# Token tiles 2 and 3 by one transposing load instead of TensorE turns, at the start of a gated mixing kernel

## The chip, the cores and the metric

The kernel runs on one core of a Trainium2 chip. The metric is the device time of one execution in microseconds (us), the median of several runs. Beside it there is one profiled execution of the kernel before, with its own time; every duration below comes from that one.

## The reference: what is computed

For 2048 tokens `x` of width 512 (32 heads of 16) two branches are computed and mixed with a gate per token. All inputs are bf16; the entries are small random numbers.

```python
g = sigmoid((x * gate_w).sum(-1, keepdims=True))
# branch A: linear attention with a learned feature map, wqkv = [wq | wk | wv]
q, k, v = split(x @ wqkv)                       # 32 heads of 16
pq, pk = q @ w_phi[h], k @ w_phi[h]             # per head, 16x16
phi = concat(softmax(p), softmax(-p))           # 32 features per head
kv, z = sum_s phi_k * v, sum_s phi_k            # over all 2048 tokens
a = ((phi_q @ kv) / (phi_q . z + 1e-6)) @ wo
# branch B: a dense layer with relu
b = relu(x @ w1) @ w2                           # 512 -> 1376 -> 512
return g * a + (1 - g) * b
```

## The kernel before

**A list of tasks with a fixed order.** Every piece of work is a named task (`add`, line 93) on one engine: SP, POOL, ACT, DVE or PE. The order of the tasks on each engine is written out by hand in `ORDER` (lines 17 to 62); `emit` (line 133) walks through an engine's string, waits for the tasks that the next one depends on, and issues it. An engine never overtakes: whatever stands behind a waiting task waits too. The `dur`, `lat` and `boost` numbers at the tasks are a planner's costs and priorities; they take no part when the kernel runs, since the order is given. `g.follow` only asserts an order.

**Layout.** `XT` holds x transposed: 128 partitions, 4 row steps (of the 512 input columns), 2048 tokens. It is filled in four chunks of 512 tokens. Chunks 1 to 3 come by transposing loads (`load_t`, line 276: `x1`, `x2`, `x3`, lines 308 to 311), which read token rows from memory and write them turned. Chunk 0, four tiles of 128 tokens, comes otherwise: `load_x` (line 287) fetches the rows of tile m plainly into `XN` (a piece of the later buffer `FT`), TensorE turns each 128x128 block by a matmul against the identity (`pe_xt`, line 348, tasks `xt{m}{n}`, two blocks each), and ACT (n = 0) and DVE (n = 1) copy the result from PSUM to `XT` (tasks `xe{m}{n}`, lines 361 to 366; 128x256 elements each).

**The start.** The first tasks of the SP queue are the loads `x00 w1a0 w1a2 x02 x03 w1b wphi wkT w1c wv x1 x2 wqT x3`; those of ACT's queue are `x01 w1a1 w1a3`. `w1a0` to `w1a3` are the four row steps of the first 512 columns of W1 (128 KB each), `w1b` the next 512 columns, `wphi` the 16x16 maps, `wkT` the key weights by a transposing load. `x1` waits until `w1c` has landed.

PE starts with `warm0` (line 257), six matmuls of 512 columns on constants whose result nobody reads. Then come `xt00 xt01 xt10 xt11`, the turns of tiles 0 and 1, and the W1 products of these two tiles: `hh00` (row step 0, tile 0), `hh01` (row step 0, tile 1), `hh1`, `hh2`, `hh3` (row steps 1 to 3, both tiles at once). Each is `pe_h_first` (line 401): four matmuls, one for each of the first four groups of 128 hidden columns, into four PSUM banks. Between `hh2` and `hh3` stand the turns of tiles 2 and 3, `xt20` to `xt31`. After `hh3` come `h0_0` to `h0_3` (`pe_h_rest`, line 407: the same four groups for tiles 2 and 3, four matmuls of 256 columns each), `h0_4`, `h0_5` (512 columns, these need `w1b`), and then `f1_0` to `f1_3` (`pe_fold`, line 372, L374): w_phi folded into the key weights, 16 matmuls, which need `wkT`.

**The rest.** From there on PE goes in its order through the W1 products `h{c}_{k}` (L397), values `v{m}` (L476), projections `pr_k`, `pr_q` (L496), sums over tokens `kv{m}` (L557), then per tile of 128 tokens the second dense layer `b{m}` (L622), the attention product `nd{m}` (L600) and the output product `a{m}` (L628). Between them POOL subtracts and multiplies for the softmaxes (L536, L550, L573; `t1`, `t2`, `nm` tasks), ACT exponentiates and empties PSUM, DVE reduces. Around the late PE tasks stand two small SP transposes per tile: `tq{m}` (L576) turns the query features from `FT` to `PHQ`, which `nd{m}` reads, and `to{m}` (L614) turns the attention result from `OTM` to `OT`, which `a{m}` reads. SP issues `tq0 tq1`, a gate store `g1_3`, then `to0 tq2`.

Of the kernel before, what the change touches and what calls it, by code (L numbers as in the profile page):

```python
# [18 lines left out]
        "x00 w1a0 w1a2 x02 x03 w1b wphi wkT w1c wv x1 x2 wqT x3 gw g1_1 g2_1 w2a g1_0 g1_2 w2b wo g2_0 tq0 tq1 "  # L19
        "g1_3 to0 tq2 tq3 to1 tq4 tq5 to2 to3 tq6 to4 tq7 g2_3 to5 g2_2 tq8 to6 tq9 to7 tq10 tq11 to8 to9 tq12 "  # L20
        "to10 tq13 tq14 to11 tq15 to12 to13 to14 to15 st15_1 "
    ),
    "pool": (
        "iota_r iota_i iota_c ones t1_k0 t2_k0 t1_k1 t2_k1 t2_k2 t1_k2 t1_k3 t2_k3 nm_k0 nm_k1 t1_k5 t1_k4 t2_k4 "
        "nm_k2 nm_k3 t1_k6 t1_k7 t2_k7 t2_k5 nm_k4 t1_k8 t2_k6 t2_k8 nm_k5 t2_q0 t1_q0 nm_k6 t2_q1 t1_q1 nm_k7 "
        "ra_q0 nm_q0 nm_k8 t2_q2 t1_q2 ra_q1 nm_q1 t1_q3 t2_q3 ra_q2 nm_q2 t1_q4 t2_q4 ra_q3 nm_q3 t1_q5 t2_q5 "
        "ra_q4 nm_q4 t2_q6 t1_q6 ra_q5 nm_q5 t2_q7 t1_q7 t2_q8 t1_q8 ra_q6 nm_q6 ra_q7 nm_q7 ra_q8 nm_q8 "
    ),
    "act": (
        "x01 w1a1 w1a3 xe00 xe10 xe20 xe30 rl0_0 rl0_1 rl0_3 rl0_2 fe1_1 fe1_3 rl0_5 rl0_4 ev_k0 rl0_8 rl0_6 "  # L30
        "rl0_7 ev_k1 rl1_0 rl0_9 ev_k2 rl1_1 ex_k0 ev_k3 rl1_3 rl1_2 ve0 rl1_5 ex_k1 rl1_4 ve1 ev_k4 rl1_6 rl1_7 "
        "ex_k3 rl1_8 ev_k5 ex_k2 ve2 rl0_10 rl1_9 ev_k6 rl1_10 ve3 rl2_0 rl2_1 ve4 ex_k4 rl2_2 ev_k7 rl2_3 rl2_4 "
        "ve5 rl2_6 rl2_5 rl2_7 ve6 rl2_8 rl2_9 rl2_10 ve7 ex_k5 ev_k8 ge1 ve8 ge0 ex_k7 rl3_0 rl3_1 ve9 ev_q0 "
        "ex_k6 ve10 gp0 ev_q1 rl3_3 ex_k8 gp1 rl3_2 rl3_4 ve11 ev_q2 ex_q0 rl3_5 ve12 ev_q3 ve13 rl3_6 ve14 ev_q4 "
        "rl3_7 ex_q1 rl3_8 ve15 rl3_9 rl3_10 ex_q2 ev_q5 ex_q3 ev_q6 oe0 ev_q7 ex_q4 oe1 st1 oe2 st0 oe3 ex_q5 "
        "ge3 ev_q8 oe4 st3 oe5 ge2 st2 ex_q6 gp2 oe6 ex_q7 st5 st4 ex_q8 st6 oe7 oe8 gp3 oe9 st7 oe10 st9 st10 "
        "oe11 st8 st11 oe12 oe14 st12 oe13 st14 st13 oe15_0 st15_0 "
    ),
    "dve": (
        "ident shift xe01 xe11 xe21 xe31 blk row4 wbd1 wbd3 mk wbd2 wbd0 fe1_0 fe1_2 mx_k0 mn_k0 mx_k1 mn_k1 "  # L40
        "mn_k2 mx_k2 mx_k3 mn_k3 sm_k0 rc_k0 sm_k1 rc_k1 mn_k4 mx_k4 mx_k5 sm_k2 gr0 rc_k2 gr1 mx_k6 sm_k3 rc_k3 "
        "mn_k7 sm_k4 mx_k7 rc_k4 mn_k5 gr2 fe0_0 fe0_1 fe0_2 fe0_3 mn_k6 mx_k8 mn_k8 sm_k5 rc_k5 mn_q0 mx_q0 "
        "sm_k6 rc_k6 sm_k8 go1 go0 sm_k7 mn_q1 mx_q1 rc_k7 sm_q0 mx_q2 rc_q0 rc_k8 mx_q3 mn_q3 mn_q2 mx_q4 sm_q1 "
        "kn1 kn0 kz0 kz1 rc_q1 mn_q4 gr3 rd0_1 rd0_0 o0_0 o0_1 sm_q2 rd1_0 rd1_1 rc_q2 mx_q5 o1_1 o1_0 mn_q5 "
        "rd2_0 rd2_1 o2_0 o2_1 sm_q3 rd3_1 rd3_0 rc_q3 o3_1 o3_0 mn_q6 rd4_1 o4_1 rd4_0 o4_0 sm_q4 rd5_0 rd5_1 "
        "rc_q4 o5_0 o5_1 mx_q6 rd6_1 rd6_0 o6_1 o6_0 sm_q5 rd7_1 rc_q5 o7_1 rd7_0 mx_q7 o7_0 mx_q8 mn_q8 mn_q7 "
        "rd8_0 rd8_1 o8_0 o8_1 sm_q6 rd9_1 rd9_0 rc_q6 o9_0 o9_1 rd10_1 rd10_0 o10_0 sm_q7 go2 o10_1 sm_q8 rd11_1 "
        "rd11_0 o11_0 rc_q8 o11_1 rc_q7 rd12_0 rd12_1 o12_1 o12_0 rd13_0 go3 rd13_1 o13_1 o13_0 rd14_0 rd14_1 "
        "o14_0 o14_1 rd15_0 rd15_1 o15_0 o15_1 oe15_1 "
    ),  # L50
    "pe": (
        "warm0 xt00 xt01 xt10 xt11 hh00 hh01 hh1 hh2 xt20 xt21 xt30 xt31 hh3 h0_0 h0_1 h0_2 h0_3 h0_4 h0_5 f1_0 "
        "f1_1 f1_2 f1_3 h0_6 pr_k0 h0_7 h0_8 pr_k1 h0_9 h1_0 pr_k2 h1_1 h1_2 pr_k3 h1_3 v0 h1_4 h1_5 v1 h1_6 "
        "pr_k4 h1_7 h1_8 v2 pr_k5 h1_9 kv0 h0_10 kv1 pr_k6 h1_10 v3 kv2 h2_0 h2_1 kv3 v4 pr_k7 h2_2 v5 h2_3 h2_4 "
        "h2_5 h2_6 h2_7 v6 h2_8 h2_9 h2_10 kv4 kv5 f0_0 kv6 f0_1 v7 f0_2 pr_k8 f0_3 h3_0 kv7 h3_1 v8 pr_q0 v9 "
        "h3_2 h3_3 v10 kv8 pr_q1 kv9 h3_4 v11 kv10 pr_q2 h3_5 kv11 v12 pr_q3 h3_6 v13 kv12 h3_7 v14 kv13 pr_q4 "
        "h3_8 h3_9 v15 kv14 h3_10 pr_q5 kv15 b0 nd0_0 nd0_1 b3 nd1_0 nd1_1 b2 pr_q6 a0 nd2_0 nd2_1 b1 nd3_1 pr_q7 "
        "nd3_0 b4 nd4_1 nd4_0 a1 pr_q8 nd5_1 a2 nd5_0 a3 b5 nd6_0 nd6_1 b7 nd7_0 nd7_1 a4 a5 b6 nd8_1 nd8_0 a6 b9 "
        "nd9_0 nd9_1 b8 nd10_0 nd10_1 a7 b10 nd11_1 a8 nd11_0 a9 b11 a10 nd12_0 nd12_1 b13 nd13_1 nd13_0 b12 "
        "nd14_0 nd14_1 b14 nd15_0 nd15_1 a11 a12 a13 a14 b15 a15_0 a15_1 "  # L60
# [88 lines left out]
def bass_gated_mix__linear_kernel_hedgehog__dense_activation_relu__prompt_kernel(  # L149
# [11 lines left out]
    x2 = A_x.rearrange("b s d -> (b s) d")  # L161
# [4 lines left out]
    P = 128  # L166
# [17 lines left out]
    WARM = (6 * (512,),)  # L184
# [3 lines left out]
    with ExitStack() as es:  # L188
# [98 lines left out]
        def load_x(m, eng, lat):  # L287
            load(f"x0{m}", eng, XN[:, m, :], x0r[:, m, :], dur=0.45, lat=lat)

        def load_w(j, eng, lat):  # L290
            load(f"w1a{j}", eng, W1[:, j, 0:512], w1r[:, j, 0:512], dur=0.45, lat=lat)

        load_x(0, "sp", 2.95)
        load_x(1, "act", 3.1)
        load_w(0, "sp", 3.2)
        load_w(1, "act", 3.4)
        load_w(2, "sp", 3.8)
        load_w(3, "act", 3.95)
        load_x(2, "sp", 4.0)
        load_x(3, "sp", 3.9)  # L300
        load("w1b", "sp", W1[:, :, 512:1024], w1r[:, :, 512:1024], dur=0.5, lat=5.0)
        load("wphi", "sp", WPS[:, :, :], A_w_phi.rearrange("(g hl) r c -> (hl r) g c", g=ND), dur=0.5, lat=4.9)
        load_t("wkT", WT[:, ND:2 * ND, :], A_wqkv[:, D:2 * D], (), 4.1, 2.7)
        load("w1c", "sp", W1[:, :, 1024:DFF], w1r[:, :, 1024:DFF], dur=0.5, lat=4.0)
        load("wv", "sp", WV[:, :, :], wvr, dur=0.5, lat=4.9)
# [40 lines left out]
        XB, FB = ((0, 1), (6, 7), (0, 1), (6, 7)), (0, 1, 6, 7)  # L346
# [7 lines left out]
        for m in range(4):  # L354
            for n in range(2):
                add(f"xt{m}{n}", "pe", lambda q, m=m, n=n: pe_xt(q, m, n),
                    (f"x0{m}", "ident", f"xe{m - 2}{n}" if m > 1 else None), dur=0.2, boost=9000.0 - 10 * m)
            for n, eng in enumerate(("act", "dve")):
                xo = XT[:, 2 * n:2 * n + 2, m * P:(m + 1) * P]
                xi = PS[:, XB[m][n], 0:2 * P].rearrange("p (j t) -> p j t", j=2)  # L360
                if eng == "act":
                    add(f"xe{m}{n}", eng, lambda q, o=xo, i=xi: q.activation(o, i, ACT.Copy), (f"xt{m}{n}",), dur=0.35,
                        boost=9000.0 - 10 * m)
                else:
                    add(f"xe{m}{n}", eng, lambda q, o=xo, i=xi: q.tensor_copy(o, i), (f"xt{m}{n}",), dur=0.37,  # L365
                        boost=9000.0 - 10 * m)
        x0 = [f"xe{m}{n}" for m in range(4) for n in range(2)]
# [10 lines left out]
        for j in range(ND):  # L378
            b = FB[j]
            war = [f"xe{2 + j // 2}{j % 2}"]  # L380
            add(f"f1_{j}", "pe", lambda q, j=j, b=b: pe_fold(q, 1, j, b), ("wkT", *wbd, *war), dur=0.24,
                boost=1800.0)
            evict(f"fe1_{j}", ("dve", "act")[j % 2], WP[:, 1, j, :], b, (f"f1_{j}",), boost=1800.0)
# [23 lines left out]
        def pe_h_rest(q, k):  # L407
            for j in range(ND):
                last = q.matmul(PS[:, GB4[k], 256:512], W1[:, j, k * P:(k + 1) * P], XT[:, j, 256:512],  # L409
                                start=(j == 0), stop=(j == ND - 1))  # L410
            return last
# [3 lines left out]
        add("hh00", "pe", lambda q: pe_h_first(q, 0, 0, P), ("xe00", "w1a0"), dur=0.22, boost=8500.0)  # L415
        add("hh01", "pe", lambda q: pe_h_first(q, 0, P, 2 * P), ("xe10", "hh00"), dur=0.22, boost=8500.0)
        prev = "hh01"
        for j in range(1, ND):
            add(f"hh{j}", "pe", lambda q, j=j: pe_h_first(q, j, 0, 2 * P), (f"xe0{j // 2}", f"xe1{j // 2}", f"w1a{j}", prev), dur=0.44,
                boost=8500.0)  # L420
            prev = f"hh{j}"
        for line in (("warm0", "xt00", "xt01", "xt10", "xt11", "hh00", "hh01", "hh1", "hh2", "xt20", "xt21", "xt30", "xt31",
                      "hh3"), ("xe00", "xe10", "xe20", "xe30"),
                     ("ident", "shift", "xe01", "xe11", "xe21", "xe31", "blk", "row4", "mk")):
            for a, b in zip(line, line[1:]):
                g.follow(a, b)
# [15 lines left out]
        for n, (kind, a, k) in enumerate(units):  # L442
            b = GB4[n] if n < 4 else HB[(n - 4) % len(HB)]
            if kind == "h":
# [5 lines left out]
                add(f"h{a}_{k}", "pe", lambda q, a=a, k=k, b=b, h=halved: pe_h_rest(q, k) if h else pe_h(q, a, k, b),  # L450
# [50 lines left out]
        for jn, (kind, tiles) in enumerate(jobs):  # L501
# [37 lines left out]
            if jn == NF - 2:  # L539
                war += [f"xt{m}{n}" for m in range(4) for n in range(2)]  # L540
# [200 lines left out]
```

## Time and profile before

| | us |
|---|---|
| median of 3 runs | 152.26 (151.87 to 152.49) |
| the profiled execution | 151.63 |
| its span, first to last instruction | 150.1 |
| PE busy | 145.3 (97%) |
| POOL, DVE, ACT busy | 109.4, 113.3, 92.2 |
| first turn on PE, `xt00` | starts at 3.57 |
| first product of tiles 2 and 3, `h0_0` | starts at 7.31 |

Times inside a profile count from the first instruction. 1.5 us of the profiled execution lie outside the span (151.63 less 150.1). In the timeline, a row gives start, duration, engine, line, operation, output<-input, shape and how many instructions of a kind were merged; in brackets stands the engine's idle time before the row and what ended it. "SPq" and "ACTq" rows are DMA issues: their duration is that of the issuing, not of the transfer. "PEld" is the loading of weights into TensorE, which runs beside its matmuls. A few matmul records are missing, which looks like a short idle stretch on PE that nothing ended.

### The profile page before, as it was taken

The page shows a single profiled execution, that of the slowest core. Times are in us where ns is not written, and L with a number is a line of the kernel's source. Part 1 is how long each engine was busy: PE and PEld are TensorE (multiplying, and loading weights), DVE is VectorE, ACT ScalarE, POOL GpSimd, SP SyncE. Part 2 cuts the span into 40 slices and gives each one's busy share as a digit, 9 for nine tenths or more (in the row PEclk, how much of TensorE's full clock was granted, in tenths as well). Part 3 has the DMA queues.
Part 4 walks back from the last instruction along what each step waited for, and adds up shares of the span by engine and source line. Part 5 has one row for each costly group of instructions (what it writes and reads, how often), then busy time and mean ns, then how long its engine had stood idle before and what let it go on. Part 6 is the DMA issues. An engine that isn't in the chain of part 4 may idle for free.

```text
span 150.1 us, 2498 instructions
## 1 busy us (share of the span) xinstructions
PE 145.3 (97%) x936; PEld 74.3 (49%) x953; DVE 113.3 (76%) x168; ACT 92.2 (61%) x127; POOL 109.4 (73%) x71
## 2 busy tenths in 40 slices
PE   7999999999999999999999999999999999999992
PEld 2774444445554465445444545455444454454461
DVE  2423666999899949969999999999999969436301
ACT  3356769799969766599983937446564551310151
POOL 3000499999999999999999999998999791330000
PEclk9999999999999999999999999999999999999999
DMA  4999991000005603400000230975659884766251
GB/s 144 302 261 239 163 231 23 0 0 0 7 1 112 238 0 54 120 0 0 4 0 0 60 82 15 116 159 135 174 106 155 195 213 105 146 171 144 65 163 52
DMA packets 46307, 15.59 MB, mean 104 GB/s; under 512 B 39796, under 2 KB 46292, under 8 KB 46296
## 3 DMA queue, kind: packets, MB, share of 16 engines
q1 hardware_dynamic: 43560, 12.99, 42.1%
q10 hardware_dynamic: 2736, 2.45, 5.0%
q8 instruction: 7, 0.11, 0.3%
q14 instruction: 4, 0.03, 0.1%
HBM read 4.42 MB, written 2.11 MB: 43 GB/s over the span
## 4 chain that ended last, share of the span: by engine, by line
PE 94%; DMA 2%; issue 1%; DVE 1%
PE PS L622 24%; PE PS L397 23%; PE PS L496 18%; PE PS L476 9%; PE PS L628 9%; PE PS L557 3%; PE PS L600 3%; DMA FT<-in_A_x_dram 2%; PE PS L643 2%; PE PS L409 1%; PE PS L374 1%; PE PS L403 1%; PE PS L350 1%; PE PS L654 1%; DVE XT L365 1%
## 5 line engine op out<-in xcount | busy, mean ns | idle before, releaser
L536 POOL TENSOR_TENSOR TS<-PB,MX 128x1024 bf16<-128x1024 bf16 (+1 forms) x18 | 30.8, 1719 | 14.9 <-DVE MX L527 14.9
L397 PE MATMUL PS<-XT,W 128*128 128x512 bf16 (+1 forms) x156 | 38.3, 379 | 0.2
L622 PE MATMUL PS<-W,HT 128*128 128x512 bf16 (+1 forms) x160 | 37.5, 379 | 0.3
L543 DVE TENSOR_REDUCE ZB<-FT 128x128 f32<-128x2048 bf16 (+1 forms) x18 | 36.5, 2030 | 0.7 <-ACT FT L541 0.6
L541 ACT ACTIVATE FT<-TS 128x2048 bf16<-128x2048 bf16 (+1 forms) x18 | 30.9, 1718 | 7.7 <-POOL TS L536 7.5
L536 POOL TENSOR_TENSOR TS<-MN,PB 128x1024 bf16<-128x1024 bf16 (+1 forms) x18 | 30.9, 1723 | 0.8 <-DVE MN L529 0.8
L496 PE MATMUL PS<-WP,XT 128*128 128x512 bf16 x124 | 30.0, 379 | 0.2
L550 POOL TENSOR_TENSOR FT<-FT,SC 128x2048 bf16<-128x2048 bf16 (+1 forms) x9 | 29.5, 3286 | 0.0
L454 ACT ACTIVATE HT<-PS 128x512 bf16<-128x512 f32 (+1 forms) x44 | 24.7, 597 | 6.1 <-PE PS L397 4.9
L622 PEld LDWEIGHTS PS<-W,HT 128*128 128x128 bf16 (+1 forms) x165 | 15.5, 98 | 17.1
L527 DVE TENSOR_REDUCE MX<-PB 128x64 bf16<-128x1024 bf16 (+1 forms) x18 | 19.5, 1084 | 5.8 <-ACT PB L523 5.7
L397 PEld LDWEIGHTS PS<-XT,W 128*128 128x128 bf16 (+1 forms) x160 | 15.6, 101 | 16.5
L673 ACT ACTIVATE OSB<-PS,OMG 128x512 bf16<-128x512 f32 x15 | 10.2, 686 | 22.1 <-PE PS L628 22.1
L529 DVE TENSOR_REDUCE MN<-PB 128x64 bf16<-128x1024 bf16 (+1 forms) x18 | 19.3, 1083 | 2.6 <-ACT PB L523 2.6
L523 ACT ACTIVATE PB<-PS 128x1024 bf16<-128x1024 f32 (+1 forms) x18 | 16.7, 926 | 6.4 <-PE PS L496 3.4
L496 PEld LDWEIGHTS PS<-WP,XT 128*128 128x128 bf16 x128 | 12.1, 98 | 13.9 <-DVE WP L344 0.4
L573 POOL TENSOR_TENSOR FT<-FT,SR 128x1024 bf16<-128x1024 bf16 (+1 forms) x9 | 15.6, 1735 | 0.7
L476 PE MATMUL PS<-WV,XT 128*128 128x512 bf16 x62 | 16.0, 379 | 0.1
L628 PE MATMUL PS<-WO,OT 128*128 128x512 bf16 x58 | 14.2, 378 | 0.1
L609 DVE SCALAR_TENSOR_TENSOR OTM<-PS,EG,RD 128x256 bf16<-128x256 f32 x32 | 13.8, 462 | 0.2
L607 DVE RECIPROCAL RD<-PS 128x16 f32<-128x16 f32 x32 | 6.5, 234 | 9.0 <-PE PS L600 8.8
L485 ACT ACTIVATE VS<-PS 128x512 bf16<-128x512 f32 x16 | 9.6, 602 | 4.8 <-PE PS L476 4.7
(50 smaller groups left out, 97.5 us busy)
## 6 DMA issues: line engine op xcount, KB each, us to landing
out_dram<-OSB ACTq DMA_DIRECT2D x15, 128.0 KB, 2.2
W<-in_B_w_dram SPq DMA_DIRECT2D x1, 1280.0 KB, 6.9
W<-in_B_w_dram SPq DMA_DIRECT2D x1, 512.0 KB, 4.6
WV<-in_A_wqkv_dram SPq DMA_DIRECT2D x1, 512.0 KB, 4.6
WO<-in_A_wo_dram SPq DMA_DIRECT2D x1, 512.0 KB, 5.1
FT<-in_A_x_dram SPq DMA_DIRECT2D x3, 128.0 KB, 3.2
W<-in_B_w_dram SPq DMA_DIRECT2D x1, 352.0 KB, 3.8
W<-in_B_w_dram ACTq DMA_DIRECT2D x2, 128.0 KB, 3.3
```

Of the source, the lines that this page charges most:

```text
L397: last = q.matmul(PS[0:m, b, :], W1[:, j, k * P:k * P + m], XT[:, j, chunk(c)], start=(j == 0), stop=(j == ND - 1))
L454: add(f"rl{a}_{k}", "act", lambda q, a=a, k=k, b=b, rows=rows: q.activation(HT[0:rows, k, chunk(a)], PS[0:rows, b, :], ACT.Relu), (prev,), ...
L476: last = q.matmul(PS[:, 2, :], XT[:, j, m * P:(m + 1) * P], WV[:, j, :], start=(j == 0), stop=(j == ND - 1))
L496: last = q.matmul(PS[:, n, :], XT[:, j, m * P:(m + 1) * P], WP[:, s, j, :], start=(j == 0), stop=(j == ND - 1))
L527: add(f"mx_{J}", "dve", lambda q, sl=sl, w=w, i=pbg: q.tensor_reduce(MX[:, sl, 0:w * H], i, AX.X, ALU.max), (f"ev_{J}", old("t1")), dur=0. ...
L529: add(f"mn_{J}", "dve", lambda q, sl=sl, w=w, i=pbg: q.tensor_reduce(MN[:, sl, 0:w * H], i, AX.X, ALU.min), (f"ev_{J}", old("t2")), dur=0. ...
L536: add(f"{tn}_{J}", "pool", lambda q, o3=o3, a3=a3, b3=b3: q.tensor_tensor(o3, a3, b3, ALU.subtract), (f"{'mx' if sg == 0 else 'mn'}_{J}", ...
L541: add(f"ex_{J}", "act", lambda q, fs=fs, ts=ts, w=w: q.activation(FT[:, fs, 0:w * F], TS[:, ts, 0:w * F], ACT.Exp), (f"t1_{J}", f"t2_{J}", ...
L543: add(f"sm_{J}", "dve", lambda q, fs=fs, sl=sl, w=w: q.tensor_reduce(ZB[:, sl, 0:2 * w * H], FT[:, fs, 0:w * F].rearrange("p (g d) -> p g ...
L550: add(f"nm_{J}", "pool", lambda q, f3=f3, sl=sl, w=w: q.tensor_tensor(f3, f3, SC[:, sl, 0:2 * w * H].unsqueeze(2).to_broadcast([P, 2 * w * ...
L622: last = q.matmul(PS[:, ab, :], HT[0:r, k, m * P:(m + 1) * P], W2[0:r, k, :], start=(k == 0), stop=False)
L628: last = q.matmul(PS[:, ab, :], OT[:, m % NOT, t, :], WO[:, t, :], start=False, stop=(t == ND - 1))
```

## The change

- The loads and turns of tiles 2 and 3 go: `x02`, `x03`, `xt20` to `xt31`, `xe20` to `xe31`. In their place there is one transposing load, `x023`, from 256 token rows straight into `XT`, in SP's queue behind `w1a2`.
- Tile 0's load `x00` becomes two loads of 64 rows each, `x00a` first in SP's queue and `x00b` first in ACT's, so that ACT issues four loads before anything else.
- The products of tiles 0 and 1 are split by tile for row step 1 as well: `hh10`, `hh11` in place of `hh1`. `hh01` stands behind the turns of tile 1 and behind `hh10`.
- The matmuls on constants are five of 512 columns and one of 256 ahead of the turns of tile 0 (`warm0`), and one of 256 columns between these turns and `hh00` (`warm1`).
- All five strings of `ORDER` are rewritten. Beside the names that go and come, tasks change places among their neighbours along the whole kernel: `h0_7` now stands ahead of `pr_k0`, `v0` ahead of `h1_0`, `kv14` and `h3_10` directly ahead of `kv15`. The order `b0, nd0, b3, nd1, b2, pr_q6, a0, nd2` on PE is as before; on SP the gate store `g1_3` moves from ahead of `to0 tq2` to behind them.
- The planner's numbers at the loads change with it; they have no part in the run.

```diff
     "sp": (
-        "x00 w1a0 w1a2 x02 x03 w1b wphi wkT w1c wv x1 x2 wqT x3 gw g1_1 g2_1 w2a g1_0 g1_2 w2b wo g2_0 tq0 tq1 "
-        "g1_3 to0 tq2 tq3 to1 ...
+        "x00a w1a0 w1a2 x023 w1b wphi wkT w1c wv x1 x2 wqT x3 gw g1_1 g1_0 g2_0 w2a w2b wo g2_1 tq0 tq1 to0 tq2 "
+        "g1_3 tq3 to1 ...
     "act": (
-        "x01 w1a1 w1a3 xe00 xe10 xe20 xe30 rl0_0 rl0_1 rl0_3 rl0_2 fe1_1 ...
+        "x00b x01 w1a1 w1a3 xe00 xe10 rl0_0 rl0_1 rl0_2 rl0_3 rl0_4 fe1_1 ...
     "pe": (
-        "warm0 xt00 xt01 xt10 xt11 hh00 hh01 hh1 hh2 xt20 xt21 xt30 xt31 hh3 h0_0 h0_1 h0_2 h0_3 h0_4 h0_5 f1_0 "
-        "f1_1 f1_2 f1_3 h0_6 pr_k0 h0_7 h0_8 pr_k1 h0_9 h1_0 pr_k2 ...
+        "warm0 xt00 xt01 warm1 hh00 xt10 xt11 hh10 hh01 hh11 hh2 hh3 h0_0 h0_1 h0_2 h0_3 h0_4 h0_5 f1_1 f1_2 f1_3 "
+        "f1_0 h0_6 h0_7 pr_k0 h0_8 h0_9 pr_k1 v0 h1_0 pr_k2 ...
-    WARM = (6 * (512,),)
+    WARM = (5 * (512,) + (256,), (256,))
-        load_x(0, "sp", 2.95)
-        load_x(1, "act", 3.1)
...
-        load_x(2, "sp", 4.0)
-        load_x(3, "sp", 3.9)
+        for n, eng in enumerate(("sp", "act")):
+            rows = slice(n * 64, n * 64 + 64)
+            load(f"x00{'ab'[n]}", eng, XN[rows, 0, :], x0r[rows, 0, :], dur=0.45, lat=1.95)
+        load_x(1, "act", 2.85)
...
+        load_t("x023", XT[:, :, 2 * P:4 * P], x2[2 * P:4 * P, :], (), 1.2, 3.0)
-        for m in range(4):
+        for m in range(2):
             for n in range(2):
                 add(f"xt{m}{n}", "pe", lambda q, m=m, n=n: pe_xt(q, m, n),
-                    (f"x0{m}", "ident", f"xe{m - 2}{n}" if m > 1 else None), dur=0.2, boost=9000.0 - 10 * m)
+                    (*(("x00a", "x00b") if m == 0 else (f"x0{m}",)), "ident"), dur=0.2, boost=9000.0 - 10 * m)
-        x0 = [f"xe{m}{n}" for m in range(4) for n in range(2)]
+        x0 = [*(f"xe{m}{n}" for m in range(2) for n in range(2)), "x023"]
-        add("hh00", "pe", lambda q: pe_h_first(q, 0, 0, P), ("xe00", "w1a0"), dur=0.22, boost=8500.0)
-        add("hh01", "pe", lambda q: pe_h_first(q, 0, P, 2 * P), ("xe10", "hh00"), dur=0.22, boost=8500.0)
-        prev = "hh01"
-        for j in range(1, ND):
+        for j in range(2):
+            for m in range(2):
+                add(f"hh{j}{m}", "pe", lambda q, j=j, m=m: pe_h_first(q, j, m * P, (m + 1) * P),
+                    (f"xe{m}0", f"w1a{j}", "hh00" if j + m else None, "hh01" if j + m == 2 else None,
+                     "hh10" if j + m == 2 else None), dur=0.22, boost=8500.0)
+        prev = "hh11"
+        for j in range(2, ND):
```

## The prediction

> **What bounds it now.** The page's busy shares come first: PE is busy for 97% of the span, and the chain that ended last is PE for 94%. The next question is whether PE ever waits, so the waits view comes next, for PE and for its weight loads (engine, line, waited for: total us, times, longest).
>
> ```profile
> PE PS L258 <- PEq L726: 0.8, 1, 0.8
> PE PS L409 <- DVE XT L365: 0.2, 1, 0.2
> ```
> ```profile
> PEld PS L350 <- DMA FT<-in_A_x_dram: 1.0, 1, 1.0
> PEld PS L409 <- ACT XT L362: 0.4, 1, 0.4
> PEld PS L496 <- DVE WP L344: 0.4, 1, 0.4
> PEld PS L600 <- DMA PHQ<-FT: 0.2, 1, 0.2
> ```
>
> Every wait of PE itself lies in the first 7.31 us; from `h0_0` (L409) to its end PE works without a stall. The other short gaps are missing records (L496: 124 matmuls, 128 weight loads). So the time is the moment at which `h0_0` starts, plus a fixed stretch of PE work, plus any new stall. The change can win only before `h0_0`, and the reordering behind it can only lose. The chain of waits up to there:
>
> ```profile
> 0.74 2.78 DMA FT<-in_A_x_dram
> 3.52 0.05 issue
> 3.57 0.97 PE PS L350 x8
> 4.53 0.30 PE PS L403 x4
> 4.83 0.03 issue
> 4.86 1.27 PE PS L403 x12
> 6.13 0.24 PE PS L350 x4
> 6.37 0.02 issue
> 6.40 0.78 DVE XT L365 x2
> 7.18 0.14 issue
> 7.31 1.91 PE PS L409 x16
> ```
>
> A load, turns, products, turns again, and at 6.37 the copies of tiles 2 and 3: their own load landed at 6.26 (issued at 2.63, 3.63 under way), just ahead of the last turns. The queues beside it:
>
> ```profile
> 2.15 0.91 SPq L272 DMA_DIRECT2D FT<-in_A_x_dram  x2
> 3.10 0.43 SPq L272 DMA_DIRECT2D W<-in_B_w_dram  x1
> 3.58 0.51 SPq L272 DMA_DIRECT2D WPS<-in_A_w_phi_dram  x1
> 4.13 3.54 SPq L277 DMA_TRANSPOSE WT<-in_A_wqkv_dram  x1
> ```
> ```profile
> 1.17 0.97 ACTq L272 DMA_DIRECT2D W<-in_B_w_dram  x2
> 2.17 1.28 ACT L362 ACT_TABLE_LOAD   x1 [2.17 <-issue]
> 4.00 0.81 ACT L362 ACTIVATE XT<-PS 128x256 bf16<-128x256 f32 x2 [0.55 <-PE PS L350]
> ```
>
> To be seen here: ACT loads its table only after its last DMA issue.
>
> **The start, step by step.** *Half loads.* The full tile took 2.78 us on SP and 2.98 (tile 1) on ACT. The windows view gives 349 GB/s for 3.57 to 4.39, so 64 KB less per queue, with two queues sharing, is 128 KB/349 = 0.37 us sooner: 3.15 to 3.3. The constants end at about 0.77 + 5 x 0.43 + 0.21 = 3.1. So `xt00` starts near 3.3, not 3.57.
>
> *ACT.* But ACT now issues four loads, so its table load starts 0.43 later, at 2.60, and ends at 3.88. `xe00` starts at 3.90 instead of 4.00, takes 0.38, and `hh00` starts 0.06 behind it: 4.34 instead of 4.44. The table load thus eats most of what the half loads bring. `w1a0` landed at 4.11 and has less ahead of it now.
>
> A rule speaks against the halves: the Trainium skill, "DMA: Bandwidth & Descriptors", section "Rules for kernel authors", says two transfers to disjoint partition halves aren't worth it, since they share the same engines. By that rule `xt00` stays at 3.57 and the gain below shrinks by the 0.10 of `hh00`; no run here shows it yet.
>
> *PE from `hh00` on.* Full-clock spacings: 0.056 to 0.06 us for 128 columns, 0.109 for 256. `hh00` takes 0.24 (0.05 more if its first matmuls still run at half speed): 4.63. `xt10`, `xt11`: 4 x 0.056, to 4.85. Tile 1 has landed (issued 0.43 later than before's 0.74, so 3.72 + 0.4 = 4.1). `hh10` runs to 5.08; `w1a1`, third on ACT's queue instead of second, lands 64 KB x 2 later, 4.31 + 0.37 = 4.68, in time. `hh01` needs `xe10`: first turn 4.63, copy 0.31 behind it (as 5.97 to 6.28 before), 0.38 long, 0.06 to the matmul: 5.38. Then `hh01` and `hh11` at 0.23 each, 5.84, and `hh2`, `hh3` at 0.435 each: 6.71. `w1a3` lands at 5.18 + 0.37 = 5.55, in time. So PE is ready for `h0_0` at 6.71 instead of 7.31: **0.60 us**. Gone are eight turns (0.45) and the wait for their copies (0.17 at PE); left is 0.3 of waiting for `xe10`.
>
> **The transposing load.** No row shows 256 token rows. Bounds: `x3` (512 KB, otherwise free queue) landed 4.45 after issue; half the bytes at the 278 GB/s of the window 13.60 to 14.80 (`x1`) is 0.94 less: 3.51, so 2.15 + 3.51 = 5.66. From above: `x2` took 5.91, so 8.06; `wkT` behind two loads took 5.62, so 7.77. I take the nearest row, the plain loads it replaces: same bytes, same place in the queue, landed at 6.26, plus 0.94 - 0.75 (256 KB at 349) = 0.19: 6.45. That leaves 0.26 before 6.71.
>
> *Behind it on SP* stand `w1b`, `wphi`, `wkT`. Its issue is half of `x1`'s 1.79, 0.9 us, what the two plain issues took together (0.91); at half of `wkT`'s 3.54 it is 0.9 longer. `w1b` landed at 7.70 and is needed at 6.71 + 1.75 = 8.46. `wkT` landed at 9.75; at the same rates it moves to 9.94, and `f1` wants it at 8.46 + 8 x 0.216 = 10.19. Slack 0.25; a late issue of 0.9 would make a stall of at most 0.65. `x1` landed at 17.13 and `h1_0` wants it near 18.7 as before, since `v0` now stands ahead of it.
>
> **The late part.** PE 0.60 earlier eats into slack everywhere. POOL begins its softmaxes after `pr_k0`, which has one unit more ahead of it (0.86) and so ends 0.26 later; POOL then works without a gap up to `nm_q1`, 92.21 + 0.26 = 92.47. The thinnest place is tile 2 (issues on SP, weight loads on PE):
>
> ```profile
> 92.37 1.20 SPq L614 DMA_TRANSPOSE OT<-OTM  x1
> 93.61 3.61 SPq L576 DMA_TRANSPOSE PHQ<-FT  x2
> ```
> ```profile
> 96.85 0.69 PEld L628 LDWEIGHTS PS<-WO,OT 128*128 128x128 bf16 x4 [0.17 <-issue]
> 97.77 0.40 PEld L600 LDWEIGHTS PS<-KVN,PHQ 128*128 128x128 bf16 x8 [0.22 <-DMA PHQ<-FT]
> ```
>
> `to0` (issued 92.37, 4.38 to landing) and `tq2` (93.61, 4.11) landed at 96.75 and 97.72, each just as PE asked. Others take 2.4 and 2.8: a 16 KB fetch of instructions at 94.38 lies in between. `tq2` was issued right behind `to0`, and `to0` hangs on `nd0` of PE, so both issues move forward with PE (91.77 and 93.0, past `nm_q1`): `nd2` wants data at 97.17, they land at 97.1 if 4.11 holds. I cost this at nothing; if the fetch holds the landing at 97.72, 0.55 is lost.
>
> **Sum.** 151.63 - 0.60 = 151.03 for the profiled execution, which is 0.63 under the median of the runs shown; on that median 152.26 - 0.60 = 151.66, say 151.7. About 0.5% (0.76 us) is what a measurement of this kernel can tell from no change, so this gain is below it.
>
> **Rivals.**
> - *Gain lost again* (0.21): `nd2`, `nd0` behind a later `kz1`, or `f1` stalls, 0.2 to 0.6: 151.9 to 152.2. For: slack of 0.25 and less. Against: the issues move with PE.
> - *The transposing load is late* (0.14): landing at 7.77 puts `h0_0` at 7.85: 152.8; at `x2`'s 5.91, 8.12: 153.1. It decides from 6.71 on. Against: `x2` and `wkT` carried twice the bytes.
> - *The clock stays low* (0.07, slower). PE starts at half speed: the six matmuls of 512 columns stand 0.427 apart, later ones 0.216, and the change comes at about 4.4, 3.6 us after PE's first work, although the granted clock reads 1.00 all along. Before, PE idles 0.29 of these 3.6 (3.28 to 3.57). Now: 0.2 ahead of `xt00`, and `warm1` ends at 3.3 + 0.43 + 0.21 = 3.94, 0.4 ahead of `hh00`; 0.6 in all. If that is too much and the switch comes 3.6 later, at 8.0, the work in between takes twice as long: 1.8, less 0.3 of waiting that it fills: 152.26 - 0.6 + 1.5 = 153.2. It decides at the idle share, 0.08 before, 0.17 now. The Trainium skill, "TensorE: Matmul & The Clock Gate", Part 1, names such a switch: a free-running window of about 3.4 us, the transition varying by half a microsecond. By it one window more would be the price; the trace agrees with its 3.6.
> - *More* (0.10): table load earlier than I think, `hh00` at 4.1, `x023` at 6.4: 0.9 gained, 151.4.
> - *As forecast* (0.48): 151.4 to 151.9.
>
> **Range and chances.** From 151.2 (the larger gain, less a scatter of 0.2) to 152.9 (lost gain, and the milder half of the late load); outside remain the clock, the worse late load and scatter. Faster by over 0.5% (under 151.5): 0.10 plus a quarter to a third of the forecast's 0.48, 0.24. Slower by over 0.5%: 0.07 and most of the late load, 0.16. Within: 0.60.
>
> **What would show it.** Right: `xt00` near 3.3, table load ending near 3.9, `h0_0` near 6.7 with no DMA wait, no wait of PE from there on. Wrong: L409 waiting for a DMA of XT (load late); L374 waiting for WT; spacings of 0.1 for 128 columns beyond 4.6 (clock); L600 or L628 waiting for `PHQ` or `OT` (gain lost late).

## The result, and the profile after

The changed kernel takes 158.1 us (median of 6 runs, 156.92 to 160.37), the kernel before 152.3 us beside it on the same chip (6 runs, 151.84 to 152.52): a ratio of 1.0365, with a 95% interval from 1.032 to 1.0409. The ratio leaves out the longest of the six runs (160.37), which lies more than 1.5% above the shortest. The forecast was 151.7, so it was wrong by 6.4 us and in sign, and 158.1 lies far outside its range.

The profiled execution of after took 158.24 us with a span of 156.4 (before: 151.63 and 150.1). Two starting times and the end of PE's work locate the difference. `f1` is the first task that needs `wkT`; from it to PE's last matmul the two kernels do the same PE work.

| us | before | after | difference |
|---|---|---|---|
| `h0_0` starts | 7.31 | 8.67 | +1.36 |
| `f1` starts | 10.78 | 12.37 | +1.59 |
| from `f1` to the end of PE's last matmul | 136.47 | 141.39 | +4.92 |
| from there to the end of the span | 2.85 | 2.64 | -0.21 |

So 1.59 us were lost at the start, and three times as much somewhere behind, where the prediction had expected nothing. The waits of PE and of its weight loads say where (engine, line, waited for: total us, times, longest):

```profile
PEld PS L481 <- ACT VS L490: 3.7, 1, 3.7
PE PS L481 <- ACT VS L490: 3.2, 1, 3.2
...
PE PS L405 <- DMA W<-in_B_w_dram: 0.9, 1, 0.9
```

To be seen here: one single wait of 3.2 us at a value product (`v`, L481; before it was L476, the new lines shift by five), for ACT to empty a PSUM bank. Before, PE had no wait at all behind 7.31. ACT is only the messenger. The chain of waits through this stretch (start, us, what):

```profile
46.28 0.50 SPq L272
...
46.83 0.69 SPq L272
...
47.55 0.52 SPq L272
...
48.12 7.16 DMA GL<-gate_scratch
...
55.30 0.21 ACT EG L441
55.51 0.48 ACT HT L459
55.99 0.50 ACT VS L490
...
56.54 1.57 PE PS L481 x4
```

SP issues `w2a`, `w2b` and `wo` (1280, 96 and 512 KB, 1.9 MB together) and only then `g2_1`, the load of one gate back from memory, 2 KB. It took 7.16 us to land. The gate load ahead of the three, `g2_0`, landed 2.14 after its issue at 45.84. On ACT `ge1` (L441), the exponential with which that gate's sigmoid begins, waited 3.93 us for it, and behind `ge1` stand `rl2_5` and `ve5`, which empty the banks that PE wants. Before, `g2_1` stood ahead of the weights, here in SP's timeline:

```profile
44.95 0.38 SPq L433 DMA_DIRECT2D GL<-gate_scratch  x1
45.38 0.50 SPq L272 DMA_DIRECT2D W<-in_B_w_dram  x1
```

It landed at 47.07, and `ge1` came only at 60.20.

The stall has a tail. The windows view of after (from:to, length, busy time by engine, then the granted clock, DMA share and GB/s) for the 3.6 us behind the stall and a stretch after them:

```profile
56.60:60.20 3.60, 3.60 (x17) 1.65 (x18) 2.62 (x4) 2.38 (x5) 0.73 (x1) 0.54 0.00 0
60.60:64.00 3.40, 3.40 (x25) 1.84 (x24) 1.66 (x3) 1.66 (x5) 3.40 (x3) 1.00 0.02 5
```

Behind 3.2 us of idle PE the granted clock is 0.54 for 3.6 us: 17 matmuls of PE in the first window, 25 in the shorter second. At 0.54 about 3.6 x 0.46 = 1.7 us are lost. (The trace's own record of the clock says 0.5 from 56.91 to 60.32, and 1.00 on both sides of it.) The stall itself moved the next matmul by 3.38 us (56.54 instead of 52.95 + 0.216); with the 4.92 of the table that leaves 1.54 for the clock, which fits.

Now the start. The chain up to `h0_0` (L411):

```profile
0.73 0.58 SPq L272
...
1.37 3.35 DMA W<-in_B_w_dram
...
4.86 0.58 PE PS L405 x4
5.44 0.43 PE PS L352 x4
5.87 3.00 PE PS L405 x20
8.88 1.93 PE PS L411 x16
```

The chain begins with the issue of the half load `x00a`, 0.58 us, which moves the issue of `w1a0`, the first W1 step, from 1.21 to 1.37. The chain names `w1a0` because it came last, at 4.72; ACT was as late. Its timeline:

```profile
0.74 1.28 ACTq L272 DMA_DIRECT2D FT<-in_A_x_dram  x2
2.06 0.94 ACTq L272 DMA_DIRECT2D W<-in_B_w_dram  x2
3.03 1.28 ACT L364 ACT_TABLE_LOAD   x1 [3.03 <-issue]
4.32 0.38 ACT L364 ACTIVATE XT<-PS 128x256 bf16<-128x256 f32 x1
```

The first row holds two issues, the half tile and tile 1: 1.28 together, where before the one load of tile 1 took 0.40. The table load starts at 3.03, not at 2.17, and the first copy of turned columns at 4.32, after which `hh00` could start at 4.76 at the earliest. PE, idle for 0.86, then does the products `hh` at half speed: 128-column matmuls about 0.11 apart until 9.1.

### The profile page after: what moved, and what is told of

Same layout as the page of the kernel before. It is cut to its first block, busy times and chain, and to the rows that moved or that the text cites. A ratio compares the mean times of both kernels' runs of the same rounds, so it can differ in the third digit from the quotient of the medians.

```text
span 156.4 us, 2503 instructions
## 1 busy us (share of the span) xinstructions
PE 148.9 (95%) x950; PEld 75.9 (49%) x950; DVE 112.8 (72%) x166; ACT 91.3 (58%) x125; POOL 109.3 (70%) x71
## 3 DMA queue, kind: packets, MB, share of 16 engines
HBM read 4.15 MB, written 2.11 MB: 40 GB/s over the span
## 4 chain that ended last, share of the span: by engine, by line
PE 87%; DMA 7%; SPq 2%; ACT 1%; DVE 1%; issue 0%
PE PS L627 23%; PE PS L399 19%; PE PS L501 17%; PE PS L633 8%; PE PS L481 8%; DMA GL<-gate_scratch 5%; PE PS L605 3%; PE PS L562 3%; PE PS L405 2%; DMA W<-in_B_w_dram 2%; PE PS L648 2%; SPq L272 1%; PE PS L411 1%; PE PS L376 1%; DMA gate_scratch<-GROW 1%; PE PS L659 1%
## 5 line engine op out<-in xcount | busy, mean ns | idle before, releaser
L399 PE MATMUL PS<-XT,W 128*128 128x512 bf16 (+1 forms) x160 | 39.6, 386 | 0.0
L627 PE MATMUL PS<-W,HT 128*128 128x512 bf16 (+1 forms) x165 | 38.1, 379 | 0.0
L501 PE MATMUL PS<-WP,XT 128*128 128x512 bf16 x128 | 30.6, 379 | 0.0
L481 PE MATMUL PS<-WV,XT 128*128 128x512 bf16 x64 | 17.0, 389 | 3.2 <-ACT VS L490 3.2
```

The costliest lines, as they stand in the source:

```text
L399: last = q.matmul(PS[0:m, b, :], W1[:, j, k * P:k * P + m], XT[:, j, chunk(c)], start=(j == 0), stop=(j == ND - 1))
L481: last = q.matmul(PS[:, 2, :], XT[:, j, m * P:(m + 1) * P], WV[:, j, :], start=(j == 0), stop=(j == ND - 1))
L501: last = q.matmul(PS[:, n, :], XT[:, j, m * P:(m + 1) * P], WP[:, s, j, :], start=(j == 0), stop=(j == ND - 1))
L627: last = q.matmul(PS[:, ab, :], HT[0:r, k, m * P:(m + 1) * P], W2[0:r, k, :], start=(k == 0), stop=False)
```

## The experiments

My theory: two causes that have nothing to do with each other. (1) The moved gate load and the earlier `ge1` make the stall and its slow clock, some 4 us. (2) The half loads make the late start. Rivals: the stall comes from other parts of the reordering; the start is late because of the transposing load, or because of the clock alone. The table sums up all the runs; ratios are against the kernel before on the same chip, medians in us.

| run | median | ratio (95%) | `f1` starts | `f1` to PE's end |
|---|---|---|---|---|
| e1_gates_first | 153.66 | 1.0095 (1.0061 to 1.013) | 12.99 | 136.35 |
| e2_start_alone | 153.34 | 1.0082 (1.0054 to 1.0111) | 12.27 | 136.47 |
| e3_gates_moved_in_before | 157.9 | 1.0376 (1.0335 to 1.0418) | 11.41 | 142.38 |
| e4_longer_warm | 153.04 | 1.0072 (1.0049 to 1.0095) | 11.93 | 136.35 |
| e5_no_halves | 151.6 | 0.997 (0.9953 to 0.9987) | 10.76 | 136.36 |
| e6_halves_in_before | 153.79 | 1.0127 (1.0095 to 1.0159) | 12.35 | 136.47 |
| e7_w1a3_ahead | 152.51 | 1.003 (1.0009 to 1.0051) | 12.14 | 136.36 |
| e8_w1a3_ahead_old_order | 152.66 | 1.0038 (1.002 to 1.0056) | 11.95 | 136.48 |
| e9_halves_on_sp | 153.44 | 1.0073 (1.005 to 1.0095) | 12.62 | 136.35 |
| e10_halves_by_columns | 151.75 | 0.9976 (0.9958 to 0.9994) | 11.20 | 136.36 |
| e11_w1b_split | 151.55 | 0.9955 (0.9936 to 0.9974) | 11.03 | 136.35 |

The last column is the quickest reading of all: it is 136.35 to 136.48 in every kernel but two, after (141.39) and e3, and these two alone have the gate load `g2_1` behind the weights. What else the runs differ in happens ahead of `f1`.

**The gate load.** In e1, on the changed kernel, one name moves:

```diff
-  ... gw g1_1 g1_0 g2_0 w2a w2b wo g2_1 tq0 ...
+  ... gw g1_1 g1_0 g2_1 g2_0 w2a w2b wo tq0 ...
```

> The changed kernel with one move on SP: the load g2_1 goes ahead of w2a, w2b and wo instead of behind them. Theory (two separate losses: 1.6 us at the start, and 3.4 us of stall plus 1.3 us of low clock behind it, because ge1 on ACT waits for g2_1 and g2_1 lies behind 1.9 MB of weights): g2_1 lands near 48, no wait of PE at L481, 158.1 - 4.7 = 153.4 us. Rival (the stall comes from the new place of ge1 on ACT, not from the place of the load): a wait of ACT for GL of over 1 us stays, 155 us or more.

Measured: 153.66 against 152.01, +1.65 where after had +5.8. The two gate loads are issued together, ahead of the weights:

```profile
46.13 0.94 SPq L437 DMA_DIRECT2D GL<-gate_scratch  x2
47.11 1.23 SPq L272 DMA_DIRECT2D W<-in_B_w_dram  x2
```

They landed 2.12 and 2.48 after issue, the wait at L481 is gone, and the granted clock stays at 1.00. Some 4 of the 5.8 us are this one place in a queue (4.15 by the medians, 4.1 by the ratios). `ge1` keeps its early place here (and `f1` to PE's end is 136.35), so that place alone costs nothing.

e3 does the opposite: only the gates move, in the kernel before.

```diff
 sp
-  ... g1_1 g2_1 w2a g1_0 g1_2 w2b wo g2_0 tq0 ...
+  ... g1_1 g1_0 g2_0 w2a w2b wo g2_1 g1_2 tq0 ...
 act
-  ... rl2_4 ve5 rl2_6 ... ex_k5 ev_k8 ge1 ve8 ge0 ex_k7 ...
+  ... rl2_4 ge1 ve5 ge0 rl2_6 ... ex_k5 ev_k8 ve8 ex_k7 ...
```

> The kernel before with only the gate tasks moved to their new places: on SP g2_1 behind w2a, w2b and wo; on ACT ge1 and ge0 around ve5 instead of around ve8. Theory: the same stall at L476 of about 3.4 us, with or without a low clock behind it: 152.3 + 3.4 to 4.7 = 155.7 to 157 us. Rival (the stall needs the rest of the new order): under 153 us.

Measured: 157.9 against 152.01, +5.9, more than expected. Its waits:

```profile
ACT EG L437 <- DMA GL<-gate_scratch: 5.8, 2, 5.1
...
PE PS L476 <- ACT VS L485: 3.8, 1, 3.8
```

The same two waits as in after, at the lines of before: a gate load of 7.52 us, ACT held for 5.1, PE for 3.8, and behind it the 512-column matmuls stand 0.427 apart from 57.4 to 61. A reordering that leaves every instruction as it was is worth 5.9 us. Cause (1) is shown from both sides. No run moves the load alone; `ge1` at its place of before, 60.20, would not have waited for a landing at 55.56, so by this estimate it takes both moves.

**The start.** e2 takes the new start (half loads, `x023`, split row steps, the shorter `warm0` with `warm1`) and leaves everything behind it in the order of before:

```diff
 sp
-  x00 w1a0 w1a2 x02 x03 w1b ... g1_1 g2_1 w2a ...
+  x00a w1a0 w1a2 x023 w1b ... g1_1 g2_1 w2a ...
```

> The kernel before with the new start only (half loads, transposing load, split row step 1, the two pieces of constant matmuls); every other place in the order is as before. Theory: the start alone costs 1.6 us, because hh00 waits to about 4.86 for w1a0 and PE then runs at half speed to about 9: 152.3 + 1.6 = 153.9 us, h0_4 near 10.6 instead of 9.06. Rival (the start is worth what was forecast and the loss lies in the reordering alone): 151.7 us. Second rival (the low clock at the start is an accident of one execution): between 152.0 and 152.8 us.

Measured: 153.34 against 152.01, +1.33, less than the theory's 153.9 and above its second rival's 152.8. So the start alone makes the kernel slower. It ran at full speed from `hh00` on, and yet `h0_0` came at 8.8, since `hh3` waited for `w1a3`, which landed at 8.30, and `f1` at 12.27. The late start doesn't need a late clock.

e4 goes at the clock directly, by more matmuls on constants between the turns and `hh00` (on e1):

```diff
-    WARM = (5 * (512,) + (256,), (256,))
+    WARM = (5 * (512,) + (256,), (256, 512, 512))
```

> The changed kernel with g2_1 ahead of the weights, and the second piece of constant matmuls longer: 256 and twice 512 columns instead of 256, so that PE has work from the turns of tile 0 to hh00. Theory (idle of 1.07 us before hh00 keeps PE at half speed up to about 9): the spacing of 128-column matmuls falls to 0.056 by about 4.6, h0_0 near 7.3 instead of 8.67, 152.3 us, 1.3 under the kernel that differs in this piece alone. Rival (the switch has nothing to do with this idle time): same time as that kernel, 153.4 us, spacings of 0.107 up to about 9.

Measured: 153.04 against 152.01, where 152.3 was expected: a miss. Full speed came at 5.0 instead of e1's 9.7, but PE then waited 1.0 us for `w1a3`, landed at 7.96. Against e1 the median is 0.6 us better, which the overlapping intervals don't tell from nothing (in the two profiled executions `f1` comes 1.06 sooner). What is left of the late start in e4 is waiting for data.

e6 puts the half loads alone into the kernel before:

```diff
-        load_x(0, "sp", 2.95)
+        for n, eng in enumerate(("sp", "act")):
+            rows = slice(n * 64, n * 64 + 64)
+            load(f"x00{'ab'[n]}", eng, XN[rows, 0, :], x0r[rows, 0, :], dur=0.45, lat=1.95)
```

> The kernel before with the half loads of tile 0 and nothing else. Theory (the halves cost issue time on ACT): table load ends near 4.4, hh00 near 4.9 instead of 4.4, h0_0 at 7.8 or later, 152.5 us or more, up to 153.5 if the longer idle of PE also keeps it slow. Forecast's view: 0.10 us faster than before. View that two halves share the engines and change nothing: 152.0 us.

Measured: 153.79 against 152.19, +1.6, a little above what was expected, with no transposing load and with full speed from 4.4 on. ACT's timeline:

```profile
0.74 1.47 ACTq L272 DMA_DIRECT2D FT<-in_A_x_dram  x2
2.24 0.94 ACTq L272 DMA_DIRECT2D W<-in_B_w_dram  x2
3.21 1.28 ACT L364 ACT_TABLE_LOAD   x1 [3.21 <-issue]
```

`w1a1` landed at 6.09, `hh00` started at 4.94, `h0_0` at 8.88. e5 is the counterpart: the changed kernel with e1's edit, tile 0 whole again on SP, and `WARM = (6 * (512,), (256,))`; `x023` stays.

> The changed kernel with g2_1 ahead of the weights, and tile 0 again as one load on SP, so that ACT issues three loads; constants six times 512 columns, then 256 behind the turns. Theory (the half loads cost: each takes ACT and SP 0.57 us to issue instead of 0.41, the next on ACT 0.85, so the table load ends at 4.3 to 4.5 instead of 3.45 and holds xe00 and hh00 back to 4.94; w1a3 is issued at 2.7 instead of 1.7): hh00 at 4.4 to 4.5, full speed by about 4.6, h0_0 held by x023 or w1a3 at 7.3 to 7.8, 152.2 to 152.6 us, at least 1 us under the kernel with the halves (153.66). Rival (the halves cost nothing, the loss is the transposing load's alone): 153.4 us or more.

Measured: 151.6 against 152.19, faster than before by 0.3% (0.13 to 0.47%), better than the 152.2 to 152.6 expected, and 2.2 us better than e1 (each against its own before). ACT's table load and SP's transposing load:

```profile
2.17 1.28 ACT L362 ACT_TABLE_LOAD   x1 [2.17 <-issue]
```
```profile
2.15 1.34 SPq L277 DMA_TRANSPOSE XT<-in_A_x_dram  x1
```

`x023` landed at 6.43, `h0_0` started at 6.75. Cause (2) is shown from both sides as well, and the transposing load isn't it. (e5 also makes `warm0` longer by 256 columns; e10 below leaves it as in after.)

**What about a half load is slow?** e9 puts both halves on SP, so that ACT issues only three loads; e10 cuts the tile by columns instead of rows, with one half on each queue, and lets each turn of tile 0 wait for its own half alone (both on e1):

```diff
 e9
-        for n, eng in enumerate(("sp", "act")):
+        for n, eng in enumerate(("sp", "sp")):
 e10
-            rows = slice(n * 64, n * 64 + 64)
-            load(..., XN[rows, 0, :], x0r[rows, 0, :], ...)
+            cols = slice(n * 256, n * 256 + 256)
+            load(..., XN[:, 0, cols], x0r[:, 0, cols], ...)
```

> The changed kernel with g2_1 ahead of the weights and both halves of tile 0 (64 rows each) on SP, so that ACT's queue has three loads as in the kernel before. Theory A (a load of 64 rows takes longer to issue than one of 128: 0.57 us instead of 0.41, and the load behind it too): SP's halves take 0.55 or more each, ACT's loads 0.41 to 0.47 again, table load at 2.17, w1a0 issued near 1.9 and landed near 4.8, hh00 near 4.9, 152.2 to 153.2 us. Theory B (the issue is slow only because ACT has one load more): SP's halves take 0.41 each, w1a0 lands near 4.5, about 151.8 us.

> The changed kernel with g2_1 ahead of the weights and tile 0 cut into two loads by columns (all 128 rows, 256 columns each), one on SP and one on ACT. Theory A (64 rows are slow to issue): these issue in 0.41 to 0.47 us, the table load starts near 2.6 and ends near 3.9, w1a3 is issued near 2.15, hh00 near 4.4, 151.6 to 152.3 us. Theory B (one load more on ACT costs as much in whatever shape): table load near 3.2 to 4.5, hh00 near 4.9, 153.3 us or more.

Measured: e9 153.44, still +1.26 on 152.18 and a little above what was expected. SP issued the halves in 0.58 and 0.57, ACT its 128-row load in 0.38, so it is the 64 rows that issue slowly, on whichever queue. The second half landed at 4.33, `hh00` came at 5.26 and full speed at 9.2. That SP now has one load more ahead of `w1a0` is part of this loss too. e10: 151.75, faster than before by 0.24% (0.06 to 0.42%). Its ACT rows:

```profile
0.75 0.91 ACTq L272 DMA_DIRECT2D FT<-in_A_x_dram  x2
...
2.65 1.28 ACT L364 ACT_TABLE_LOAD   x1 [2.65 <-issue]
```

0.91 for two issues instead of 1.28 to 1.47. `hh00` came at 4.38, one copy behind the table load, so the turns' own waits decide nothing. The same bytes in the same two loads, cut the other way, are worth 2.1 us in the medians (e1 +1.65, e10 -0.43).

**What is late next.** e7 moves `w1a3` on SP ahead of `x023` (on e5); e8 has that start with the order of before behind it.

```diff
-  x00 w1a0 w1a2 x023 w1b ...        act: x01 w1a1 w1a3 xe00 ...
+  x00 w1a0 w1a2 w1a3 x023 w1b ...   act: x01 w1a1 xe00 ...
```

> As the kernel without halves, and w1a3 is moved from ACT's queue to SP's, ahead of x023, so that no plain load is under way on the other queue while the transposing load's packets move. Theory (packets of 256 bytes of x023 beside packets of 1 KB of the other queue drop the DMA rate from about 350 to about 170 GB/s and hold w1a3 and x023 back): the rate beside x023 stays near 280 GB/s, w1a3 lands near 5.4, x023 near 6.6, h0_0 near 6.8, 151.6 us. Rival (the transposing load is slow by itself): x023 still lands 5.5 us or more after its issue, h0_0 near 8, 152.8 us.

> The same start as the kernel with w1a3 ahead, on the order of the kernel before for everything behind it. Theory: the rest of the reordering is neutral apart from the gate load, so the two agree within 0.3 us. Rival (the new order adds stalls behind the start): this one is faster by 0.5 us or more.

Measured: e7 152.51, 0.9 worse than e5 and not the 151.6 expected. `x023` itself was hardly later (6.58, 3.96 under way), but everything behind it on SP was: `w1b`, issued 0.48 later, landed at 9.93 instead of 8.64, and PE waited:

```profile
PE PS L397 <- DMA W<-in_B_w_dram: 1.4, 1, 1.4
```

Why 0.48 of issue became 1.29 of landing stays open; in e10 `w1b` was issued at 3.54 as in e5 and landed at 9.24, so some of it may be scatter. e8 gives 152.66, 0.15 from e7 and not told apart from it: apart from the gate load, the whole rewritten order is neutral within some 0.4 us, which is what these two intervals can tell.

e11 takes the waits left in e5: of `w1b`, the second half of the columns goes behind `wkT` as a load of its own.

```diff
-        load("w1b", "sp", W1[:, :, 512:1024], w1r[:, :, 512:1024], dur=0.5, lat=5.0)
+        load("w1b", "sp", W1[:, :, 512:768], w1r[:, :, 512:768], dur=0.5, lat=5.0)
...
+        load("w1d", "sp", W1[:, :, 768:1024], w1r[:, :, 768:1024], dur=0.5, lat=3.4)
```

> The kernel without half loads and with g2_1 ahead of the weights, and w1b cut in two: columns 512 to 767 where it was, columns 768 to 1023 as w1d behind wkT. Theory (in the kernel without halves the start is bound by the order of the transfers: h0_4 waits 0.3 us for w1b, f1 0.3 to 0.6 us for wkT): w1b lands near 7.9, wkT near 9.9, neither is waited for, h0_6 waits at most 0.2 us for w1d: 0.4 us less, 151.2 us. Rival (wkT waits for something other than the bytes ahead of it): wkT still lands near 10.7 and w1d later than needed, 151.6 us or more.

Measured: 151.55 against 152.29, faster by 0.45% (0.26 to 0.64%): the best of all by its ratio, but not told apart from e5, and short of the 151.2 expected. `w1b` landed at 7.80 and `wkT` at 10.01, and neither was waited for; the profiled execution, in which full speed came only at 6.6, reached `f1` at 11.03.

## Why the prediction was wrong

**The step that failed most, "The late part".** It says that the reordering behind `h0_0` "can only lose" and then costs it at nothing, after a look at one place, the transposes of tile 2. That place was as forecast: in e5 `to0` was issued at 91.71 (forecast 91.77) and `tq2` at 92.95 (93.0), which landed at 97.13 (97.1), and PE did not wait for it. But the diff moves `g2_1` past three weight loads of 1.9 MB, and `ge1` on ACT from behind `ev_k8` to ahead of `rl2_5` and `ve5`. Neither was followed, and of no moved wait was it asked what stands behind it. Some 4 of the 5.8 us are this (e1), 5.9 alone (e3). The price could have been read from before: its own gate load behind `w2b` and `wo`, `g2_0`, took 3.84 against 2.12 for the one ahead of the weights, and `ge0` waited 0.48 for it. The Trainium skill, "DMA: Bandwidth & Descriptors", section "Queues, rings and completion order", says that each DMA engine takes descriptors in the order of its ring; the runs agree, with 7.16 and 7.52 us for 2 KB behind 1.9 MB against 2.10 to 2.48 ahead of it.

**The second, "ACT": 0.43 for the fourth issue.** That was the price of a 128-row load. A 64-row load took 0.57, and the load behind it 0.68 (after) to 0.86 (e4) instead of 0.40; on SP `w1a0`, behind the other half, took 0.56 instead of 0.43. So the table load began at 3.03 (2.60 forecast), `hh00` at 4.86 (4.34; `w1a0` at 4.72 held it as well, but landed at 3.95 to 4.19 in e1, e2, e4 and e6, where `hh00` came at 4.93 to 4.94 all the same), and `w1a1` and `w1a3` landed at 5.58 and 6.31 (4.68 and 5.55). With column halves, which do cost 0.41 to 0.47, the forecast comes true: table load 2.65 to 3.93, `xe00` 3.94, `hh00` 4.38 (forecast 2.60, 3.88, 3.90, 4.34). It is a mis-sized term, but one that turned a gain into a loss: +1.6 by itself (e6).

The prediction weighed the rule of the Trainium skill, "DMA: Bandwidth & Descriptors", section "Rules for kernel authors", against partition halves and gave it 0.10 us. Its advice was right, but the shared engines are not where the runs show the loss: the halves did land sooner (2.93 and 3.11, the whole tile before at 3.52), and the loss is in the issuing.

**"The transposing load" and "Behind it on SP".** Without the halves the landing is 6.43 (forecast 6.45) and `h0_0` starts at 6.75 (6.71): 0.56 of the 0.60 are there. That the landing fits so well is in part luck, since the same load landed anywhere from 6.39 to 8.59 in these runs. In after it landed at 7.24, later than the 6.71 from which it would have decided, and in e1 and e2 at 8.59 and 8.51, beyond both landings that the rival "late load" reckoned with; but PE was late itself and `w1a3` landed at nearly the same time (8.46 and 8.30 in e1 and e2), so the load shows in no wait. The issue took 1.34, not 0.9; in e5 `wkT` landed at 10.71 (forecast 9.94) and was waited for, `w1b` at 8.64 where 8.46 was needed, and `f1` came at 10.76, where it was before (10.78). In these two profiled executions the gain of 0.56 at `h0_0` is thus given back by `f1`: the rival "gain lost again", through the loads that the prediction named. The medians differ by 0.59 all the same. Before's profiled execution was 0.6 under the median of its runs, so a usual run of before may reach `f1` later. One profile shows such a run: e3, whose start is that of before, task for task, reached `f1` at 11.41 instead of 10.78.

**"The clock stays low".** It came about, at both places. At the start of after, half speed lasted until 9.1 rather than 4.4. In that execution it was worth some 1.0 of the 1.59 us: `x023` landed at 7.24, `w1b` at 9.41 and `wkT` at 11.31, so at full speed `f1` could have started near 11.36 instead of 12.37 (an estimate from these landings). It isn't needed for the loss: e2 and e6 ran at full speed and lost 1.3 and 1.6. Behind the stall, which no rival had, it cost about 1.5.

The idle share of the 3.6 us behind PE's first work, which the prediction gave as its deciding point, doesn't decide: before, with 0.29 us idle, was at full speed by 4.4, and e3, with the same start and 0.10, only at 6.4. The traces hold something that does sort the runs, their records of the clock. All but the last of each trace last a whole multiple of 3.413 us, and the first one, at full speed, starts at 4.33 in before, 6.41 in e3 and 9.12 in after. Count back from this moment in windows of 3.413 us, and the last window ahead of it has at most 0.83 us of idle PE in all 13 profiles, every earlier one at least 1.04. (PE counts as busy for as long as the spacing of its matmuls asks at the clock of the moment, 0.427 us for 512 columns at half speed, and as idle ahead of its first. e2 has no such records; there the matmuls draw together at about 3.65.) Where the windows lie differs from one execution to the next, which is luck. But in after the window from 2.29 to 5.70 had 1.20 us idle, where the forecast had 0.6 in all, because `hh00` came at 4.86: by this count the low clock in after follows from the half loads.

Together, by differences of medians: +5.8 is 4.15 for the gate load with its slow clock, and 2.2 for the half loads (e1 to e5), less the 0.6 that remains as e5's gain.

## What to carry to other kernels

When a diff rewrites orders by hand, list for each engine and queue every wait that changed its place, and ask of each what it is now behind and what is now behind it; a look at the thinnest place of before says nothing of the places that the change makes thin. A small load that somebody waits for goes ahead of large ones in its queue, even if it isn't wanted soon. And the price of an issue is read from a row of the same shape, or bounded: here the same bytes cost 0.41 or 0.57 by the direction of the cut, and all that ACT issues at the start stands ahead of its first instruction (table load at 2.17 us in e5, 2.65 in e10, 3.03 in after, 3.21 in e6).

## What was not expected of the hardware

- A load of 64 KB to 64 partitions took 0.56 to 0.58 us to issue on SP and on ACT, one of 128 KB to 128 partitions 0.38 to 0.48, one of 64 KB to 128 partitions 0.41. The load behind a 64-row load was slow as well, 0.56 to 0.58 on SP and 0.68 to 0.86 on ACT.
- The transposing load was under way for 3.78 to 4.79 us in after, e5 and e7 to e11, and for 5.74 to 6.13 in e1, e2 and e4, where `w1a3` on the other queue was late as well (7.96 to 8.46). Between 4.8 and 7.2 us e5 moved 252 GB/s, e1 144. Which of the two holds back the other, no run separates; after and e1 have the same start and lie in different groups.
- The moment of full speed varied from about 3.65 (e2) to 9.7 us (e1) over the profiled executions. In every profile a window of 3.413 us with at most 0.83 us idle lies directly ahead of it, and no window with less than 1.04 idle lies earlier. The granted clock in the profile's rows reads 1.00 all through the slow start only because the trace has no record of the clock there (in after, none ahead of 9.12) and the profile counts that as full; behind the stall it has one, and the rows read 0.54.
- In two further executions of after the mean clock was 1.000, with spans of 155.1 and 155.5 instead of 156.4: there the same stall was followed by no slow stretch, it seems. (e2, without any clock record, reads 1.000 too, so the spans are the better sign.) The Trainium skill, "TensorE: Matmul & The Clock Gate", Part 1, calls its window free-running and the warm-up run-variable. The runs agree: the records' lengths show the window, and its place shifts from run to run.
